# Eight-row loads for the first batch of a fused attention and GLU kernel, with squares moved to ScalarE and output weights loaded later

## The chip, the cores and the metric

The kernel runs on one core of one Trainium2 chip. The metric is the device time of one execution in microseconds (us), lower is better. Quoted times are medians of several runs. A traced run gives the profile and its own time; the profile's span, from the first to the last instruction, is some 2 us shorter than that time.

## The reference

Four batches of q, k and v, each 6016 rows by 256 columns in fp32. Per batch a channel attention of 256 by 256, then a gated feed-forward over all 24064 rows:

```python
qn = q / (np.linalg.norm(q, axis=1, keepdims=True) + 1e-06)     # norm over the 6016 rows
kn = k / (np.linalg.norm(k, axis=1, keepdims=True) + 1e-06)
s = kn.transpose(0, 2, 1) @ qn / tau                             # (B, 256, 256)
a = softmax(s)                                                   # written out in the original
x = (v @ a).reshape(B * N, C)
gate = 1.0 / (1.0 + np.exp(-(x @ w_gate)))                       # w_gate, w_val: 256 x 1536
return (gate * (x @ w_val)) @ w_out                              # w_out: 1536 x 256
```

## The kernel before

The rows of a batch are laid on 128 partitions, 47 rows each, and worked in groups of four rows ("four-row group": 128 partitions x 4 rows x 256, 512 KB of fp32 in HBM, cast to 256 KB of bf16 on the way). For the first batch nothing can overlap: all of q and k must land before its softmax is known. Then `a @ w_gate` and `a @ w_val` are formed (`gh`), and the feed-forward reads v directly. While batch b runs through the feed-forward, q and k of batch b+1 are loaded and their scores and squares are squeezed in as side work.

```python
TPC = 4                                      # rows of a group
NCH = (NT + TPC - 1) // TPC                  # 12 groups, NT = 47
groups0 = groups[: head // TPC] + [...]      # first batch: 11 groups of four, then rows 44-45, then row 46
qkpool = pool("qkpool", NCH)                 # slots for q and for k, four rows each
...
def load_qk(b, t0, nt):
    tiles = []
    for name, src in (("q", q), ("k", k)):
        tl = qkpool.tile([P, TPC, C], BF16, tag=name, name=name + "_sb")
        nc.gpsimd.dma_start(out=tl[:, :nt, :], in_=rows(src, b)[:, t0 : t0 + nt, :])
        tiles.append(tl)
    qk[b, t0] = tiles
...                                          # first group: two fp32 loads on other queues, cast on chip
for t0, nt in groups0[2:]:
    load_qk(0, t0, nt)
load_v(0, 0)
for fg in range(NFG):                        # gate and value weights, three pieces each, alternating
    for w, src in enumerate((moe_w_gate, moe_w_val)):
        nc.gpsimd.dma_start(out=w_sb[w][fg], in_=...)
load_v(0, 1)
nc.gpsimd.dma_start(out=w_out_sb, in_=moe_w_out.rearrange("(t p) c -> p t c", p=P))
...
for g, (t0, nt) in enumerate(groups0):       # first batch: squares, sums, scores
    engines = (nc.vector, nc.scalar) if g < last0 else (nc.scalar, nc.vector)
    sq = [squares(0, t0, nt, w, engines[w], ...) for w in range(2)]
    ...                                      # VectorE adds the squares up
    for u in range(nt):
        score(0, t0, u)
    if n_acc - 4 <= g < n_acc:
        busy(1)                              # a filler product on TensorE
...                                          # norms, softmax, busy(3), busy(1), first products gh(0, 0..4)
```

From there on a loop over chunks of v calls, at fixed places, the side work: `load_v` two chunks ahead, `transpose_v` (a DMA transpose of the next chunk from the SyncE queue, `vT<-v_sb`) one chunk ahead, and `load_qk` for the next batch about 20 of the loop's steps before use. A load waits on GpSimd until its slot is free (in the changed kernel GpSimd stood 5.26 us before the load at 74.63 us).

Of the kernel before, what the change touches and what calls it, by code (L numbers as in the profile page):

```python
# [10 lines left out]
BF16 = mybir.dt.bfloat16  # L11
# [6 lines left out]
def kernel(  # L18
# [20 lines left out]
    nc = tc.nc  # L39
    P = nc.NUM_PARTITIONS  # L40
# [4 lines left out]
    B, N, C = q.shape  # L45
# [7 lines left out]
    TPC = 4  # L53
    CH = TPC * P
    NCH = (NT + TPC - 1) // TPC
    groups = [(t, min(TPC, NT - t)) for t in range(0, NT, TPC)]

    head = NT - NT % TPC
    groups0 = groups[: head // TPC] + [(t, n) for t, n in ((head, NT % TPC - 1), (NT - 1, 1)) if n > 0]

    def rows(x, b):
        return x[b].rearrange("(p t) c -> p t c", p=P)
# [3 lines left out]
    def pool(name, bufs, **kw):  # L66
        return ctx.enter_context(tc.tile_pool(name=name, bufs=bufs, **kw))

    consts = pool("consts", 1)
    qkpool = pool("qkpool", NCH)  # L70
    sqpool = pool("sqpool", 3)
    attp = pool("attp", 1)
    ghpool = pool("ghpool", 2)
# [17 lines left out]
    qk = {}  # L91

    def load_qk(b, t0, nt):
        tiles = []
        for name, src in (("q", q), ("k", k)):
            tl = qkpool.tile([P, TPC, C], BF16, tag=name, name=name + "_sb")
            nc.gpsimd.dma_start(out=tl[:, :nt, :], in_=rows(src, b)[:, t0 : t0 + nt, :])  # L97
            tiles.append(tl)
        qk[b, t0] = tiles

    vs = {}

    def load_v(b, ci):
        t0, nt = groups[ci]
        v_sb = vpool.tile([P, TPC, C], BF16, tag="v", name="v_sb")
        nc.gpsimd.dma_start(out=v_sb[:, :nt, :], in_=rows(v, b)[:, t0 : t0 + nt, :])  # L106
        vs[b, ci] = v_sb


    t0, nt = groups0[0]  # L110
    qk[0, 0] = [qkpool.tile([P, TPC, C], BF16, tag=n, name=n + "_sb") for n in ("q", "k")]
    first_f32 = [consts.tile([P, nt, C], FP32, name=f"first{w}") for w in range(2)]
    for eng, tl, src in zip((nc.sync, nc.scalar), first_f32, (q, k)):
        eng.dma_start(out=tl, in_=rows(src, 0)[:, t0 : t0 + nt, :])
    nc.scalar.preload_act_table(ACT.Sqrt)
    load_qk(0, *groups0[1])

    ident_bf = consts.tile([P, P], BF16)
    make_identity(nc, ident_bf)
# [8 lines left out]

    nc.vector.tensor_copy(out=qk[0, 0][0], in_=first_f32[0])
    nc.scalar.copy(qk[0, 0][1], first_f32[1])  # L130
    for t0, nt in groups0[2:]:
        load_qk(0, t0, nt)
    load_v(0, 0)

# [1 line left out]
    w_out_sb = consts.tile([P, FC, C], BF16)  # L136
    for fg in range(NFG):
        for w, src in enumerate((moe_w_gate, moe_w_val)):
            nc.gpsimd.dma_start(
                out=w_sb[w][fg],  # L140
                in_=src.rearrange("(t p) f -> p t f", p=P)[:, :, ds(fg * FG, FG)],
            )
    load_v(0, 1)
    nc.gpsimd.dma_start(out=w_out_sb, in_=moe_w_out.rearrange("(t p) c -> p t c", p=P))


    st = {}
# [5 lines left out]
    def score(b, t0, u):  # L153
        q_sb, k_sb = qk[b, t0]
        if t0 == 0 and u == 0:
            st.setdefault(b, {})["s"] = pss.tile([P, CB, C], FP32, tag="s", name="ps_s")
        ps_s = st[b]["s"]
        t = t0 + u
        for j in range(CB):
            mm(  # L160
                ps_s[:, j, :],
                q_sb[:, u, ds(j * P, P)],
                k_sb[:, u, :],
                start=(t == 0 and j == 0),
                stop=(t == NT - 1),
                skip_group_check=True,
            )

    def squares(b, t0, nt, which, engine, sq=None):
        src = qk[b, t0][which]  # L170
        if sq is None:
            sq = sqpool.tile([P, TPC, C], BF16, tag=f"sq{which}", name=f"sq{which}")
        if engine is nc.scalar:
            nc.scalar.activation(out=sq[:, :nt, :], in_=src[:, :nt, :], func=ACT.Square)  # L174
        else:
            engine.tensor_tensor(  # L176
                out=sq[:, :nt, :], in0=src[:, :nt, :], in1=src[:, :nt, :], op=ALU.mult
            )
        return sq

    def norm_mms(ps, sqs, nt, first, last, order=(0, 1)):

        for w in order:
            sq = sqs[w]
            for u in range(nt):
                for j in range(CB):
                    mm(
                        ps[:, w * CB + j : w * CB + j + 1],
                        sq[:, u, ds(j * P, P)],
                        ones_bf[:, 0:1],  # L190
                        start=(first and w == order[0] and u == 0 and j == 0),
                        stop=(last and u == nt - 1),
                        skip_group_check=True,
                    )
# [276 lines left out]
    def busy(n):  # L471

        ps = psg.tile([P, CH], FP32, tag="g", name="ps_busy")
        for _ in range(n):
            mm(ps, ones_bf, ones_wide, True, True)
# [3 lines left out]
    n_acc = NT // TPC  # L479
    acc_start(0)  # L480
    acc = st[0]["acc"]
    last0 = len(groups0) - 1
    adds, ends = [], []
    for g, (t0, nt) in enumerate(groups0):
        engines = (nc.vector, nc.scalar) if g < last0 else (nc.scalar, nc.vector)
        sq = [squares(0, t0, nt, w, engines[w], acc[w] if g == 0 else None) for w in range(2)]
        while adds:
            w, last_sq = adds.pop()
            nc.vector.tensor_tensor(out=acc[w], in0=acc[w], in1=last_sq, op=ALU.add)
        if 0 < g < n_acc:  # L490
            nc.vector.tensor_tensor(out=acc[0], in0=acc[0], in1=sq[0], op=ALU.add)
            if g < n_acc - 1:
                nc.vector.tensor_tensor(out=acc[1], in0=acc[1], in1=sq[1], op=ALU.add)
            else:
                adds.append((1, sq[1]))
        elif g:
            ends.append((sq, nt))
        if g == last0:
            norm_mms(ps_n0, acc, TPC, True, False)
            for n, (end, rows_n) in enumerate(ends):  # L500
                norm_mms(ps_n0, end, rows_n, False, n == len(ends) - 1, (1, 0) if n else (0, 1))
# [3 lines that stand above are left out]
            busy(1)  # L505
# [28 lines left out]
    def side_work(b):  # L534


        side = {}

        def at(slot, fn, *a):
            side.setdefault(divmod(slot, FC), []).append((fn, a))  # L540

        for ci in range(NCH):
            nb, nci = (b, ci + 1) if ci + 1 < NCH else (b + 1, 0)
            lb, lci = (b, ci + 2) if ci + 2 < NCH else (b + 1, ci + 2 - NCH)
            if (nb, nci) == (0, 1):
                at(8, lambda: transpose_v(0, 1, psm.tile([P, TPC * CB, P], BF16, tag="m", name="ps_tp")))
            elif nb < B:
                at(ci * FC + 2, transpose_v, nb, nci)
            if lb < B:
                at(ci * FC + 0, load_v, lb, lci)  # L550
        n = b + 1
        if n == B:
            return side
        first, last = (14 if b == 0 else 0), 8 * FC
        for g, (t0, nt) in enumerate(groups):
            s0 = first + g * (last - first) // NCH
            at(max(0, s0 - 20), load_qk, n, t0, nt)
            for u in range(nt):
                at(first + (t0 + u) * (last - first) // NT, score, n, t0, u)
            if g == 0:  # L560
                at(s0, acc_start, n)
            for i, (fn, w) in enumerate(((acc_square, 0), (acc_add, 0), (acc_square, 1), (acc_add, 1))):
                at(s0 + 1 + 2 * i, fn, n, g, w)
        for i in range(6):
            at(8 * FC + 2 + i, acc_fold, n, *divmod(i, 3))
        at(9 * FC + 9, norms_mm, n)
        for ci, s, *call in (
            (9, 0, wide_sqrt, n),
            (9, 2, wide_inv, n, 0),
            (9, 3, wide_inv, n, 1),  # L570
            (10, 0, wide_scale, n),
            (10, 0, exps, n, 0),
            (10, 0, exps, n, 1),
        ):
            side.setdefault((ci, FC + s), []).append((call[0], call[1:]))
        at(11 * FC + 0, sums_both, n)
        at(11 * FC + 0, gh_tiles, n)
        for i in range(len(gh_order)):
            at(11 * FC + min(i + 1, FC - 1), gh, n, i, *((pss, "s"), (psm, "m"))[i % 2])
        return side  # L580
# [62 lines left out]
```

## Time and profile before

| | before |
|---|---|
| time, first three runs | 829.55 us (829.47 to 829.68) |
| time, all six runs beside the changed kernel | 829.62 us (829.47 to 829.97) |
| span of the traced run (829.76 us) | 827.7 us |
| TensorE busy | 806.9 us, 97% of the span |
| first gate product starts | 36.55 us |
| first output product starts | 53.94 us |

The page's first part (engine, busy time, share, instructions), a row of its second (40 slices of the span, the DMA engines' busy share in tenths) and one of its third (DMA queues: packets, MB, share of 16 engines):

```profile
PE 806.9 (97%) x5122; PEld 498.5 (60%) x5134; DVE 591.5 (71%) x1027; ACT 390.8 (47%) x642; POOL 83.1 (10%) x159
DMA  9999623226746443223876452223322323322211
...
q0 software_dynamic: 23920, 38.81, 28.1%
```

TensorE is nearly the whole span. The DMA row is full only in its first four slices, 83 us: up to about 48 us that is the first batch's q and k and the weights, and then mostly the second batch's q and k. q0 is GpSimd's queue of loads; the transposes and the stores go by another.

### The profile page before, as it was taken

The page shows a single profiled execution, that of the slowest core. Times are in us where ns is not written, and L with a number is a line of the kernel's source. Part 1 is how long each engine was busy: PE and PEld are TensorE (multiplying, and loading weights), DVE is VectorE, ACT ScalarE, POOL GpSimd, SP SyncE. Part 2 cuts the span into 40 slices and gives each one's busy share as a digit, 9 for nine tenths or more (in the row PEclk, how much of TensorE's full clock was granted, in tenths as well). Part 3 has the DMA queues.
Part 4 walks back from the last instruction along what each step waited for, and adds up shares of the span by engine and source line. Part 5 has one row for each costly group of instructions (what it writes and reads, how often), then busy time and mean ns, then how long its engine had stood idle before and what let it go on. Part 6 is the DMA issues. An engine that isn't in the chain of part 4 may idle for free.

```text
span 827.7 us, 13626 instructions
## 1 busy us (share of the span) xinstructions
PE 806.9 (97%) x5122; PEld 498.5 (60%) x5134; DVE 591.5 (71%) x1027; ACT 390.8 (47%) x642; POOL 83.1 (10%) x159
## 2 busy tenths in 40 slices
PE   4799999999999999999999999999999999999998
PEld 2456666665665666665575666666566566666666
DVE  6777877787667777778767777777766666666665
ACT  4554444446644444445654444444655444444442
POOL 5532100002210100000311010000000000000000
PEclk9899999999999999999999999999999999999999
DMA  9999623226746443223876452223322323322211
GB/s 210 206 201 216 110 52 90 60 53 136 158 88 119 96 89 61 54 52 85 158 138 124 80 107 60 51 63 75 64 61 63 73 52 85 60 58 69 47 36 71
DMA packets 79026, 77.17 MB, mean 93 GB/s; under 512 B 50800, under 2 KB 55920, under 8 KB 78960
## 3 DMA queue, kind: packets, MB, share of 16 engines
q0 software_dynamic: 23920, 38.81, 28.1%
q1 hardware_dynamic: 54752, 36.91, 17.4%
q8 instruction: 40, 0.66, 0.3%
q10 hardware_dynamic: 288, 0.59, 0.2%
q14 instruction: 26, 0.21, 0.1%
HBM read 78.64 MB, written 24.64 MB: 125 GB/s over the span
## 4 chain that ended last, share of the span: by engine, by line
PE 94%; DMA 4%; DVE 1%; issue 0%; ACT 0%; POOL 0%; POOLq 0%
PE ps_o L88 30%; PE ps_gate L88 29%; PE ps_val L88 29%; PE ps_s L88 4%; DMA k_sb<-in_k_dram 3%; PE ps_gh L88 2%; DMA w_gate<-in_moe_w_gate_dram 1%; DVE hT L426 0%; ACT g_sb L425 0%; PE ps_end L88 0%; DVE sq L176 0%; PE ps_n L88 0%; POOL q_sb L97 0%; PE ps_tp L396 0%; DVE end L467 0%
## 5 line engine op out<-in xcount | busy, mean ns | idle before, releaser
L426 DVE TENSOR_TENSOR hT<-ps_val,g_sb 128x512 bf16<-128x512 f32 (+1 forms) x576 | 390.8, 679 | 205.6 <-ACT g_sb L425 201.0
L425 ACT ACTIVATE g_sb<-ps_gate 128x512 bf16<-128x512 f32 (+1 forms) x576 | 338.2, 588 | 386.2 <-PE ps_gate L88 380.2
L88 PE MATMUL ps_val<-vT,gh_H 128*128 128x512 bf16 (+1 forms) x1152 | 337.6, 375 | 0.3
L88 PE MATMUL ps_gate<-vT,gh_G 128*128 128x512 bf16 (+1 forms) x1152 | 337.5, 375 | 0.2
L88 PE MATMUL ps_o<-w_out_sb,hT 128*128 128x256 bf16 x2244 | 324.9, 273 | 0.0
L88 PEld LDWEIGHTS <-hT 128*128 128x128 bf16 x2268 | 221.0, 98 | 124.6
L88 PEld LDWEIGHTS <-gh_H 128*128 128x128 bf16 x1152 | 112.7, 98 | 132.1 <-issue 1.4
L88 PEld LDWEIGHTS <-gh_G 128*128 128x128 bf16 x1152 | 112.4, 98 | 37.6 <-ACT gh_G L379 0.2
L106 POOL DMA_DIRECT2D v_sb<-in_v_dram x48 | 25.5, 531 | 620.2 <-DMA vT<-v_sb 480.4
L452 DVE COPY out_sb<-ps_o 128x256 f32<-128x256 f32 x187 | 77.2, 413 | 12.6 <-PE ps_o L88 12.6
L88 PE MATMUL ps_s<-k_sb,q_sb 128*128 128x256 bf16 x376 | 70.5, 289 | 15.8 <-DMA k_sb<-in_k_dram 8.8
L88 PEld LDWEIGHTS <-q_sb 128*128 128x128 bf16 x376 | 38.6, 103 | 24.6 <-issue 9.6
L215 DVE TENSOR_TENSOR acc<-acc,sq 128x1024 bf16<-128x1024 bf16 (+1 forms) x66 | 44.1, 669 | 0.0
L176 DVE TENSOR_TENSOR sq<-q_sb 128x1024 bf16<-128x1024 bf16 (+2 forms) x44 | 29.3, 667 | 0.0
L97 POOL DMA_DIRECT2D q_sb<-in_q_dram x48 | 26.5, 552 | 15.2 <-DMA q_sb<-in_q_dram 7.3
L97 POOL DMA_DIRECT2D k_sb<-in_k_dram x48 | 26.2, 545 | 16.1 <-DMA k_sb<-in_k_dram 6.6
L176 DVE TENSOR_TENSOR sq<-k_sb 128x1024 bf16<-128x1024 bf16 (+2 forms) x34 | 22.4, 658 | 0.2 <-DMA k_sb<-in_k_dram 0.2
L174 ACT ACTIVATE sq<-k_sb 128x1024 bf16<-128x1024 bf16 (+1 forms) x11 | 11.2, 1019 | 13.6 <-DMA k_sb<-in_k_dram 13.6
L88 PE MATMUL ps_gh<-w_val,e_sb 128*128 128x512 bf16 x45 | 13.5, 379 | 0.2
L88 PEld LDWEIGHTS <-e_sb 128*128 128x128 bf16 x112 | 10.2, 98 | 5.3 <-DMA w_gate<-in_moe_w_gate_dram 0.6
L88 PE MATMUL ps_gh<-w_gate,e_sb 128*128 128x512 bf16 x41 | 12.7, 379 | 0.7 <-DMA w_gate<-in_moe_w_gate_dram 0.5
L425 ACT ACT_TABLE_LOAD x6 | 7.7, 1283 | 9.0 <-PE ps_gate L88 9.0
(69 smaller groups left out, 121.1 us busy)
## 6 DMA issues: line engine op xcount, KB each, us to landing
out_dram<-out_sb SPq DMA_DIRECT2D x44, 512.0 KB, 2.9
v_sb<-in_v_dram POOLq DMA_DIRECT2D x44, 256.0 KB, 3.8
q_sb<-in_q_dram POOLq DMA_DIRECT2D x43, 256.0 KB, 7.4
k_sb<-in_k_dram POOLq DMA_DIRECT2D x43, 256.0 KB, 8.1
out_dram<-out_sb SPq DMA_DIRECT2D x3, 384.0 KB, 3.1
w_gate<-in_moe_w_gate_dram POOLq DMA_DIRECT2D x3, 256.0 KB, 8.0
w_val<-in_moe_w_val_dram POOLq DMA_DIRECT2D x3, 256.0 KB, 8.1
w_out_sb<-in_moe_w_out_dram POOLq DMA_DIRECT2D x1, 768.0 KB, 13.3
```

The lines of the kernel that those rows point to most:

```text
L88: nc.tensor.matmul(out, lhsT=lhsT, rhs=rhs, start=start, stop=stop, **kw)
L97: nc.gpsimd.dma_start(out=tl[:, :nt, :], in_=rows(src, b)[:, t0 : t0 + nt, :])
L106: nc.gpsimd.dma_start(out=v_sb[:, :nt, :], in_=rows(v, b)[:, t0 : t0 + nt, :])
L174: nc.scalar.activation(out=sq[:, :nt, :], in_=src[:, :nt, :], func=ACT.Square)
L176: engine.tensor_tensor(out=sq[:, :nt, :], in0=src[:, :nt, :], in1=src[:, :nt, :], op=ALU.mult)
L215: nc.vector.tensor_tensor(out=acc[:, :nt, :], in0=acc[:, :nt, :], in1=st[b]["sq", w][:, :nt, :], op=ALU.add)
L425: nc.scalar.activation(out=g_sb[:, :n], in_=ps_gate[:, :n], func=ACT.Sigmoid)
L426: nc.vector.tensor_tensor(out=hts[b, ci][:, f, :n], in0=ps_val[:, :n], in1=g_sb[:, :n], op=ALU.mult)
L452: nc.vector.tensor_copy(out=out_sb[:, s, :], in_=ps)
```

## The change

The intent: fewer and larger loads where the DMA queue is the bound; ScalarE takes over two squares so that VectorE is not behind when eight rows land at once; the output weights move out of the way of what is needed sooner. The core of the diff:

```diff
-    qkpool = pool("qkpool", NCH)
+    qkpool = pool("qkpool", 8)
...
-            tl = qkpool.tile([P, TPC, C], BF16, tag=name, name=name + "_sb")
+            tl = qkpool.tile([P, 2 * TPC, C], BF16, tag=name, name=name + "_sb")
             nc.gpsimd.dma_start(out=tl[:, :nt, :], in_=rows(src, b)[:, t0 : t0 + nt, :])
             tiles.append(tl)
-        qk[b, t0] = tiles
+        for u in range(0, nt, TPC):
+            qk[b, t0 + u] = [tl[:, u : u + TPC, :] for tl in tiles]
...
+    pairs = [(t, 2 * TPC) for t in range(TPC, head - 3 * TPC, 2 * TPC)]     # rows 4 to 35
+    loads0 = pairs + [(t, n) for t, n in groups0 if t >= pairs[-1][0] + 2 * TPC]
-    load_qk(0, *groups0[1])
+    load_qk(0, *loads0[0])
...
-    for t0, nt in groups0[2:]:
+    for t0, nt in loads0[1:]:
         load_qk(0, t0, nt)
...
-    nc.gpsimd.dma_start(out=w_out_sb, in_=moe_w_out.rearrange("(t p) c -> p t c", p=P))
+    def load_w_out():
+        nc.gpsimd.dma_start(out=w_out_sb, in_=moe_w_out.rearrange("(t p) c -> p t c", p=P))
...
-        engines = (nc.vector, nc.scalar) if g < last0 else (nc.scalar, nc.vector)
+        engines = [nc.vector, nc.scalar]
+        if n_acc - 2 <= g < n_acc:
+            engines[0] = nc.scalar
+        elif g == last0:
+            engines.reverse()
...                                          # in the loop's side work:
+            if (b, ci) == (0, 0):
+                at(0, load_w_out)
```

The slots grow to eight rows for every batch, and their number falls from 12 to 8. The later batches still load four rows at a time, so each of their loads fills half a slot.

More of the change, by code (lines that the diff above doesn't have):

```diff
@@ L110 @@
     t0, nt = groups0[0]
-    qk[0, 0] = [qkpool.tile([P, TPC, C], BF16, tag=n, name=n + "_sb") for n in ("q", "k")]
+    qk[0, 0] = [
+        qkpool.tile([P, 2 * TPC, C], BF16, tag=n, name=n + "_sb")[:, :TPC, :] for n in ("q", "k")
+    ]
     first_f32 = [consts.tile([P, nt, C], FP32, name=f"first{w}") for w in range(2)]
```

## The prediction

The forecast's sum came to -0.38 us for eight larger loads and 0 for the rest, 829.2 us; the 0.38 is what "moves ahead by that" means. How GpSimd paces its loads is shown by the trace of before: eight went out by 6.39 us without a wait for a landing, and the ninth, at 7.20, waited for that of the first q load.

> **What bounds the kernel now.** I read the page first, then the chain of waits in the first 62 us, then the order of instructions there, and last the DMA queues in short windows. TensorE carries 94% of the chain that ended last, and after 36.5 us it has nothing left to give: the stretches show it busy for 25.80 of 26.00 us and for 50.00 of 50.00.
>
> ```profile
> PE 94%; DMA 4%; DVE 1%; issue 0%; ACT 0%; POOL 0%; POOLq 0%
> 36.50:62.50 26.00, 25.80 (x140) 13.16 (x142) 18.24 (x30) 15.91 (x27) 9.11 (x18) 1.00 1.20 202
> 50.00:100.00 50.00, 50.00 (x322) 31.07 (x321) 37.51 (x64) 22.37 (x38) 11.63 (x22) 1.00 1.02 182
> ```
>
> The columns of the last two are stretch, its length, then busy time of PE, PE's weight load, DVE, ACT, POOL, the granted clock, DMA share and GB/s. All that the change touches is the 4% called DMA: the first batch's q and k, and then the weights. Its chain, as start, length and what:
>
> ```profile
> 1.89 6.29 DMA k_sb<-in_k_dram
> 8.18 0.28 issue
> 8.46 9.74 DMA k_sb<-in_k_dram
> 18.20 0.28 issue
> 18.48 9.74 DMA k_sb<-in_k_dram
> 28.22 0.28 issue
> 28.51 8.00 DMA w_gate<-in_moe_w_gate_dram
> 36.51 0.05 issue
> 36.55 0.60 PE ps_gh L88 x2
> ```
>
> [...]the hop from 8.46 to 18.48 is eight loads. Then the first gate weights land at 36.51 and the first product with them starts at 36.55. From there to the end TensorE is full, so the time of this one landing is what sets the total. How tight it is against the softmax beside it:
>
> ```profile
> PE ps_gh L88 <- DMA w_gate<-in_moe_w_gate_dram: 0.5, 1, 0.5
> 32.65 0.40 ACT L174 ACTIVATE sq<-q_sb 128x256 bf16<-128x256 bf16 x1
> 32.73 0.29 DVE L176 TENSOR_TENSOR sq<-k_sb 128x256 bf16<-128x256 bf16 x1 [0.16 <-DMA k_sb<-in_k_dram]
> 35.85 0.20 PE L88 MATMUL ps_r<-ones_bf,e_sb 128*128 128x1 bf16 x2 [0.35 <-ACT e_sb L316]
> 36.55 0.60 PE L88 MATMUL ps_gh<-w_gate,e_sb 128*128 128x512 bf16 x2 [0.49 <-DMA w_gate<-in_moe_w_gate_dram]
> ```
>
> The last k row lands at about 32.7, call it L. The squares, norms, square root and exponentials are over at 36.05, and then TensorE waits 0.5 us for the gate weights. So the softmax has 0.5 us of slack, and the queue has none.
>
> [...]eight loads of 512 KB of fp32 in 10.02 us (18.48 less 8.46) is 1.2525 us each, 418.6 GB/s read. (The page's 210 GB/s counts the bf16 bytes written, half of it.) [...]the granted clock falls to 0.5 at about 18.2 us and is back at 25.0[...].
>
> **The change, part by part.**
>
> *Runs of eight rows.* Sixteen four-row loads (rows 4 to 36 of q and of k) become eight eight-row loads; three four-row groups (the first, rows 36 and 40) and the tail of two rows and one row stay. Bytes are the same. A four-row load has 128 runs of 4 KB, the new one 128 runs of 8 KB. [...]The weight loads have the same bytes in 256 runs of 2 KB; from the issues that wait for them (37.76 to 44.10, five landings, four of them weights and one v) one takes (6.34 - 1.2525) / 4 = 1.272 us. So eight more runs on each engine cost 0.020 us, 2.4 ns each. [...]Everything behind them in the queue, v and the gate weights included, moves ahead by that, as the queue is never empty: its software row is at 112% of its engines' time from 8 us on, and with eight loads in flight in place of the same eight at half the size it is fuller yet. GpSimd's 0.53 us for an issue is off the path.
>
> *Two rows of groups arriving at once.* The last eight-row pair of k lands at L - 6.9 (backwards at 1.25 us a four-row tile: k40 at L - 1.9, q40 L - 3.1, k36 L - 4.4, q36 L - 5.6). VectorE needs 3 x 0.69 us a group (q's square, two sums), and must wait for ScalarE's squares of k at 1.04 us each. Without help it would be behind for the tail; that is what the second part is for. With ScalarE taking q's squares for rows 36 and 40, I lay out the two engines. ScalarE: k28 ends at L - 5.8, k32 L - 4.75, q36 L - 3.7, k36 L - 2.7, q40 L - 1.6, k40 L - 0.6, k44 (0.63) at L, q46 (0.40) L + 0.42, against L + 0.36 before (32.65 + 0.40). VectorE: row 32's second sum L - 3.0, row 36's sums L - 2.3 and L - 1.6, row 40's first L - 0.9, q44's square (0.43) L - 0.5, row 40's second sum L + 0.2, k46's square (0.29) L + 0.5, against L + 0.33. So the softmax starts about 0.16 us later after L. That comes out of its 0.5 us of slack, and 0.34 is left: it costs nothing.
>
> *Output weights later.* They go from before to after the third v load in the same queue, behind all gate and value weights in both cases. Before, they were issued at 34.32 and landed 13.3 us later, at 47.6; now[...] about 48.5. The first product that reads them starts at 54.1. Hidden, with 5 us to spare. No gain at the first gate weights either, as they were ahead already.
>
> *Buffers.* Eight slots of eight rows in place of twelve of four for the three later batches. Load g is asked for 20 of the loop's steps before its use, with groups about 7 to 8 steps apart, so three or four groups are ahead; the slot was freed eight groups before. No wait.
>
> Sum: -0.38 for the queue, 0 for the rest: 829.55 - 0.38 = 829.2 us.[...]
>
> **Rivals.** (a) *TensorE cold at the tail.* Its scores now come in bursts 5 us apart, 16 products of 0.13 us warm. Before, with 1.03 us of work in 2.5 us (41%), it fell cold at 18.2; cold, 8 products take 1.86 us. Bursts leave idle stretches of 3 us, so it will probably be cold before the last pair at 25.5. There 16 cold products and two filler products take some 4.6 us unbroken[...] If it stays cold throughout the softmax, 831. I give these 15% together. (b) *The transfer rate does not move*[...]: 829.3 to 829.6.[...] (d) *The output weights collide*, being needed at 54.1: that takes a delay of over 5 us, and speaks against itself. (e) *Another engine's delay holds the gate weights.* They landed at 36.51, about 1.1 us later than v's cadence would put them (L + 1.25 for v + 1.25 = 35.2), and one instruction fetch ran on a DMA engine then:
>
> ```profile
> q8 instruction: 1, 0.02, 5.8%
> ```
>
> That is in the window 34 to 35 us, 5.8% of 16 us or 0.93 us on a single engine[...]; if it falls elsewhere, the landing moves by up to 1 us earlier, and then the softmax binds, at a gain of 0.38 + 0.34 at most: 828.8.
>
> **Range and chances.** Runs of before spread over 0.2 us. [...]the cold TensorE is the tail on the slow side. Range 828.6 to 829.9. 2% would be 16.6 us, and the whole stretch that the change touches is 36.5 us[...]; neither side can give 16 us. Faster 0.01, same 0.98, slower 0.01.
>
> **What the changed profile would show.** Right: eight-row loads of k land 5.01 less 0.1 us apart; the last k row near 32.3; first gate weights near 36.1 and still the thing that the first product with them waits for, by about 0.3 us; output weights landing near 48.5 with no wait for them; the stretch from there on as before. Wrong: the first product waiting for the exponentials instead (the tail of squares or a cold TensorE), the cadence unchanged at 1.25 us per four rows, or a wait on q, k or output weights after 50 us.

## The result, and the profile after

| | before | changed |
|---|---|---|
| median of six runs | 829.62 us (829.47 to 829.97) | 829.82 us (829.21 to 830.27) |
| ratio | | 1.0001, 95% interval 0.9988 to 1.0014: same |
| traced run, and its span | 829.76, 827.7 | 830.27, 828.2 |
| first gate product | 36.55 | 36.19 |
| third weight product (`w_gate`, second piece) | 38.51, no wait | 38.57, waits 0.26 |
| first output product | 53.94 | 53.78 |
| TensorE's waits for a transpose | none | one, 0.5 us (0.8 on the weight load) |

A ratio here and below is the mean time of one kernel's fast runs over that of the other's runs of the same rounds, so not quite the ratio of the medians quoted. The predicted 829.2 (828.6 to 829.9) holds the median, but the six runs spread over 1.06 us, five times what the runs of before had shown, and the traced one is the slowest of them.

The prologue first. Two lines of the timeline before, the third weight product and the first output product:

```profile
38.51 0.59 PE L88 MATMUL ps_gh<-w_gate,e_sb 128*128 128x512 bf16 x2
...
53.94 0.60 PE L88 MATMUL ps_o<-w_out_sb,hT 128*128 128x256 bf16 x4
```

The timeline of the changed kernel (start, length, engine, line, operation, count, and the idle time before it with what ended it), the scores of the first and the fourth eight-row pair, then the last k row's square, then the products with weights and the first output product:

```profile
10.64 3.57 PE L88 MATMUL ps_s<-k_sb,q_sb 128*128 128x256 bf16 x16 [1.95 <-DMA k_sb<-in_k_dram]
...
25.32 2.12 PE L88 MATMUL ps_s<-k_sb,q_sb 128*128 128x256 bf16 x16 [1.55 <-DMA k_sb<-in_k_dram]
...
32.32 0.29 DVE L184 TENSOR_TENSOR sq<-k_sb 128x256 bf16<-128x256 bf16 x1 [0.16 <-DMA k_sb<-in_k_dram]
...
36.19 0.60 PE L88 MATMUL ps_gh<-w_gate,e_sb 128*128 128x512 bf16 x2 [0.54 <-DMA w_gate<-in_moe_w_gate_dram]
...
38.57 0.59 PE L88 MATMUL ps_gh<-w_gate,e_sb 128*128 128x512 bf16 x2 [0.26 <-DMA w_gate<-in_moe_w_gate_dram]
...
53.78 0.60 PE L88 MATMUL ps_o<-w_out_sb,hT 128*128 128x256 bf16 x4
```

A pair of eight-row loads lands every (25.32 - 10.64) / 3 = 4.89 us, 2.45 us a load, against 2 x 1.2525 = 2.505 for two four-row loads in before. The last k row's square starts at 32.32 instead of 32.73, and the first gate product at 36.19 instead of 36.55. That is the predicted gain. But the second piece of `w_gate`, which before was there when TensorE came to it, is now waited for: of the 0.36 us nothing is left at 38.57 against 38.51, and 0.16 us at the first output product (53.78 against 53.94).

The chain that ended last in the changed kernel, from the page by shares of the span:

```profile
PE 92%; DMA 6%; DVE 1%; issue 0%; POOL 0%; ACT 0%; POOLq 0%
```

and piece by piece (start, length, what):

```profile
15.74 14.56 DMA k_sb<-in_k_dram
...
30.59 7.94 DMA w_gate<-in_moe_w_gate_dram
...
38.57 0.59 PE ps_gh L88 x2
...
72.62 14.98 DMA vT<-v_sb
```

It runs through the second piece of `w_gate` in place of the first. And a new link stands at 72.62: the DMA transpose of the fourth chunk of v, whose product is reached 15 us later. DMA's share of the chain is up from 4% to 6%. What waits for the transpose, from the timeline of the changed kernel:

```profile
87.64 0.60 PE L88 MATMUL ps_gate<-vT,gh_G 128*128 128x512 bf16 x2 [0.52 <-DMA vT<-v_sb]
```

The transpose was issued and landed 10.8 us later before, 15.0 after. Stretches of the two kernels (stretch, length, busy time of PE, PE's weight load, DVE, ACT, POOL, then granted clock, DMA share and GB/s), before:

```profile
78.00:82.00 4.00, 4.00 (x28) 2.63 (x27) 3.17 (x6) 1.57 (x3) 0.00 (x0) 1.00 1.17 209
...
86.00:90.00 4.00, 4.00 (x27) 2.51 (x26) 3.26 (x7) 1.79 (x3) 0.71 (x2) 1.00 1.06 196
```

and after:

```profile
78.00:82.00 4.00, 4.00 (x29) 2.52 (x27) 3.16 (x6) 1.46 (x4) 0.00 (x0) 1.00 1.38 95
...
86.00:90.00 4.00, 3.48 (x22) 1.88 (x20) 3.00 (x6) 1.39 (x3) 1.59 (x3) 1.00 0.26 28
```

TensorE loses 0.52 of 4 us at 86 to 90. From 78 to 82 the DMA engines are more occupied than before (1.38 against 1.17) but move 95 GB/s instead of 209: the packets themselves take longer. By the DMA view of that stretch a packet of the load queue took 329 ns on average instead of 151, and one of the queue of transposes and stores 80 instead of 32. What feeds them is seen on GpSimd, before:

```profile
71.42 0.53 POOL L97 DMA_DIRECT2D k_sb<-in_k_dram  x1 [0.72 <-ACT g_sb L425]
84.07 0.53 POOL L106 DMA_DIRECT2D v_sb<-in_v_dram  x1 [12.12 <-DMA vT<-v_sb]
```

and after:

```profile
68.84 0.53 POOL L98 DMA_DIRECT2D k_sb<-in_k_dram  x1 [0.68 <-DVE sq L184]
74.63 0.53 POOL L98 DMA_DIRECT2D q_sb<-in_q_dram  x1 [5.26 <-DVE hT L434]
75.15 0.54 POOL L98 DMA_DIRECT2D k_sb<-in_k_dram  x1
88.12 0.53 POOL L108 DMA_DIRECT2D v_sb<-in_v_dram  x1 [12.44 <-DVE hT L434]
```

Before, GpSimd issued the last of its loads at 71.42, ahead of the transpose. After, it stands 5.26 us, by the experiments below for want of a free slot, and issues a pair at 74.63 and 75.15, behind the transpose and into it. These two took 11.8 and 12.5 us to land.

### The profile page after: what moved, and what is told of

It is laid out like the page before. It is cut to its first block, busy times and chain, and to the rows that moved or that the text cites. A ratio compares the mean times of both kernels' runs of the same rounds, so it can differ in the third digit from the quotient of the medians.

```text
span 828.2 us, 13621 instructions
## 1 busy us (share of the span) xinstructions
PE 807.9 (98%) x5122; PEld 499.1 (60%) x5134; DVE 590.2 (71%) x1025; ACT 392.2 (47%) x644; POOL 78.9 (10%) x151
## 3 DMA queue, kind: packets, MB, share of 16 engines
q0 software_dynamic: 22768, 38.81, 28.5%
## 4 chain that ended last, share of the span: by engine, by line
PE 92%; DMA 6%; DVE 1%; issue 0%; POOL 0%; ACT 0%; POOLq 0%
PE ps_o L88 29%; PE ps_gate L88 29%; PE ps_val L88 29%; PE ps_s L88 4%; DMA k_sb<-in_k_dram 3%; PE ps_gh L88 2%; DMA vT<-v_sb 2%; DMA w_gate<-in_moe_w_gate_dram 1%; DVE hT L434 0%; DVE sq L184 0%; PE ps_end L88 0%; ACT g_sb L433 0%; POOL q_sb L98 0%; PE ps_n L88 0%; POOL k_sb L98 0%
## 5 line engine op out<-in xcount | busy, mean ns | idle before, releaser
L88 PE MATMUL ps_s<-k_sb,q_sb 128*128 128x256 bf16 x376 | 71.2, 293 | 14.6 <-DMA k_sb<-in_k_dram 7.6
L98 POOL DMA_DIRECT2D q_sb<-in_q_dram x44 | 24.2, 549 | 38.5 <-PE ps_s L88 12.4
L98 POOL DMA_DIRECT2D k_sb<-in_k_dram x44 | 24.0, 544 | 14.5 <-DMA k_sb<-in_k_dram 7.7
## 6 DMA issues: line engine op xcount, KB each, us to landing
k_sb<-in_k_dram POOLq DMA_DIRECT2D x4, 512.0 KB, 13.4
```

The lines of the kernel that those rows point to most:

```text
L88: nc.tensor.matmul(out, lhsT=lhsT, rhs=rhs, start=start, stop=stop, **kw)
```

## The experiments

Theory A: the eight slots hold GpSimd's loads back until they travel with the transpose, which then lands too late for TensorE; the prologue gains what was predicted. Rivals: the later output weights push the transpose (B); TensorE was cold at the tail, rival (a) of the prediction; the instruction fetch moved, rival (e); or the squares on ScalarE are what costs or gains. The experiments ran in three groups of four, each with the kernel before beside it (the record gives chip 0 for e1 to e8, chip 8 for e9 to e12, and no chip for the first six runs): 829.54 us (829.34 to 830.16) for e1 to e4, 829.57 (829.36 to 829.81) for e5 to e8, 829.57 (829.38 to 829.72) for e9 to e12. All results were correct.

### e1_after_again: the changed kernel, unaltered, once more

> The changed kernel unaltered, for more runs and a second trace. Its first six runs lay between 829.21 and 830.27 us. In the trace at hand the first gate product starts 0.36 us earlier than before (36.19 against 36.55 us) and then TensorE stands still once, before 87.6 us, for the transpose of the fourth v chunk, which took 15.0 us from issue to landing (10.8 before). Theory A (eight q and k slots: the loads of the second batch's later groups must wait for a slot and fall into that transpose) and rival B (the output weights' new place in the queue) both expect the same here: first gate product near 36.2, runs spread over 829.2 to 830.3, and in the traced run a wait on that transpose of 0 to 1.4 us that makes up the difference of its span from 827.1.

Measured: 829.06 us (829.02 to 829.08), ratio 0.9994 (0.998 to 1.0007). The transpose took 13.4 us and nobody waited for it. The first gate product started at 36.03, the second piece of `w_gate` was in use at 38.24, the first output product at 53.45, 0.49 us ahead of before. The spread and the wait that were expected did not come. So the same program has two outcomes, with and without the wait at 87 us, and without it the gain is in the total, though inside the noise of the ratio.

### e2_halves: sixteen groups ahead instead of eight

In the later batches two four-row groups share one eight-row slot.

```diff
+    whole = {}
     def load_qk(b, t0, nt):
+        second = b > 0 and t0 // TPC % 2 == 1
         for w, (name, src) in enumerate((("q", q), ("k", k))):
-            tl = qkpool.tile([P, 2 * TPC, C], BF16, tag=name, name=name + "_sb")
+            if second:
+                tl = whole[w][:, TPC:, :]
+            else:
+                tl = qkpool.tile([P, 2 * TPC, C], BF16, tag=name, name=name + "_sb")
+                whole[w] = tl
```

> The changed kernel, but in the later batches two four-row groups share one eight-row slot, so sixteen groups can be in flight in place of eight. Same memory. Theory A: the second batch's loads no longer wait for a slot, the transpose of the fourth v chunk lands in about 11 us as before, TensorE has no wait on it, and all runs lie at 829.2 (829.1 to 829.4), spread below 0.3. Rival B (order of the output weights): the wait stays, runs spread over 829.2 to 830.3 as for the changed kernel. Rival C (chance, unrelated to the slots): like B.

Measured: 829.14 us (829.11 to 829.40), ratio 0.9995 (0.9983 to 1.0008). GpSimd's loads ran as before the change, the last at 70.81 and the next at 83.70:

```profile
70.81 0.53 POOL L104 DMA_DIRECT2D k_sb<-in_k_dram  x1 [0.73 <-DMA k_sb<-in_k_dram]
83.70 0.53 POOL L114 DMA_DIRECT2D v_sb<-in_v_dram  x1 [12.36 <-DMA vT<-v_sb]
```

The transpose took 10.6 us. That is what A asks for. The traced run, the slowest of the five at 829.40, showed something else besides. Its stretches, in the columns given above:

```profile
28.00:30.00 2.00, 2.00 (x11) 1.19 (x10) 2.00 (x4) 2.00 (x3) 1.36 (x2) 0.50 1.11 202
30.00:32.00 2.00, 2.00 (x13) 1.46 (x12) 1.89 (x4) 1.56 (x3) 1.46 (x3) 0.69 1.30 200
```

The granted clock, third from the right, is 0.50 at 28 to 30 us where e1 has 1.00. TensorE worked through without a pause and was late with its norm products; the first gate product started at 36.38 with no wait for the weights, and the first output product at 53.76, 0.31 us behind e1. This is rival (a), at a cost of 0.3 us; the four other runs, at 829.11 to 829.18, were probably without it: their recorded mean clock is 0.996 to 1.000, that of the traced run 0.993.

### e3_wout_back: output weights at their old place

```diff
-    def load_w_out():
-        nc.gpsimd.dma_start(out=w_out_sb, in_=moe_w_out.rearrange("(t p) c -> p t c", p=P))
+    nc.gpsimd.dma_start(out=w_out_sb, in_=moe_w_out.rearrange("(t p) c -> p t c", p=P))
...
-            if (b, ci) == (0, 0):
-                at(0, load_w_out)
```

> The changed kernel with the output weights issued where they were before, ahead of the third v load. Theory A: no different from the changed kernel, a spread of 829.2 to 830.3 and q's loads still waiting for slots at about 74 us. Rival B: steady 829.2, no wait on the transpose of the fourth v chunk.

Measured: 829.32 us (829.1 to 830.37; the other four within 829.42), ratio 0.9999 (0.9986 to 1.0011). The transpose took 13.2 us, as in e1. So B falls: the order of the output weights doesn't lengthen the transpose, and the time is the same within the noise. The one run at 830.37 was not traced.

### e4_before_8slots: the kernel before with eight slots

```diff
-    qkpool = pool("qkpool", NCH)
+    qkpool = pool("qkpool", 8)
```

> The kernel before, with eight slots of four rows for q and k in place of twelve, nothing else. Theory A: the transfers of the first batch are as before (first gate product at 36.5), but the second batch's loads now wait for slots and the transpose of the fourth v chunk is late in some runs: 829.5 to 830.6, with a wider spread than before's 0.5. Rival B: like before, 829.5 to 829.9. If the first batch's own loads lose time to eight slots, the first gate product would start later than 36.6, which neither expects.

Measured: 829.43 us (829.38 to 829.66), ratio 0.9999 (0.9986 to 1.0012). The transpose took 13.7 us instead of 10.8, and GpSimd stood 5.08 us and then issued a pair at 74.70:

```profile
69.09 0.53 POOL L97 DMA_DIRECT2D k_sb<-in_k_dram  x1 [0.68 <-DVE sq L176]
74.70 0.53 POOL L97 DMA_DIRECT2D q_sb<-in_q_dram  x1 [5.08 <-DVE hT L426]
```

No product waited, and the late runs and the wider spread that A expected did not come. So it is the number of slots that lengthens the transpose, without any eight-row load; at 13.7 it is still in time. That the slots alone lead to a wait is not shown.

### e5_sq_back: q's squares of the last two groups back on VectorE

```diff
-        if n_acc - 2 <= g < n_acc:
-            engines[0] = nc.scalar
-        elif g == last0:
+        if g == last0:
             engines.reverse()
```

> The changed kernel with q's squares for rows 36 and 40 back on VectorE. By the layout in the prediction VectorE then has 2 x 0.69 us more to do after the last pair, so k46's square ends about 1.4 us later than now (33.9 in place of 32.6), the first gate product starts when the softmax is done and not when the weights land, at about 37.0 us in place of 36.15, and the time is 829.9 (829.6 to 830.3). If the prediction's claim that the squares are hidden is wrong and VectorE never was behind, nothing changes: 829.1.

Measured: 830.04 us (829.85 to 830.19), ratio 1.0006 (0.9994 to 1.0019). From the timeline:

```profile
33.20 0.35 PE L88 MATMUL ps_n<-ones_bf,acc 128*128 128x1 bf16 x8 [0.59 <-DVE acc L499]
...
36.48 0.59 PE L88 MATMUL ps_gh<-w_gate,e_sb 128*128 128x512 bf16 x2
```

The norm products wait for VectorE's sum, and the first gate product starts at 36.48 with its weights there. (37.0 was expected; the last k row's square came at 33.06 instead of 33.9.) The first output product starts at 53.87, 0.42 us behind e1. In this run the transpose took 14.9 us and TensorE's weight load waited 0.7 for it. So the ScalarE squares are needed: without them the softmax takes back the queue's gain. That the total met the expected 829.9 or so is in part luck, as it holds the wait for the transpose.

### e6_gate_later: one v load moved ahead of the weights

The second v load stands before the gate and value weights, so each of these lands one load later.

```diff
     load_v(0, 0)
+    load_v(0, 1)
...
-    load_v(0, 1)
```

> The changed kernel with the second v load moved from behind the gate and value weights to ahead of them: one four-row load (1.25 us) more in front of the weights, same bytes in all. If the landing of the weights sets the total, as the prediction has it, the first gate product starts 1.25 us later, at 37.4, and the time is 830.3 (830.1 to 830.5). If the softmax or TensorE's own work sets it, less than 0.7 us is lost: below 829.8.

Measured: 830.64 us (830.3 to 831.56), ratio 1.0018 (1.0004 to 1.0032). The timeline shows three waits on weights:

```profile
36.87 0.60 PE L88 MATMUL ps_gh<-w_gate,e_sb 128*128 128x512 bf16 x2 [1.08 <-DMA w_gate<-in_moe_w_gate_dram]
38.15 1.02 PE L88 MATMUL ps_gh<-w_val,e_sb 128*128 128x512 bf16 x4 [0.19 <-DMA w_val<-in_moe_w_val_dram]
39.47 0.59 PE L88 MATMUL ps_gh<-w_gate,e_sb 128*128 128x512 bf16 x2 [0.30 <-DMA w_gate<-in_moe_w_gate_dram]
```

The first gate product was expected at 37.4 and came at 36.87, 0.84 us behind e1 and not one load. But 39.47 against 38.24 in e1 is 1.23 us, one load, and the three runs at 830.30 to 830.64 are 1.24 to 1.58 us above e1's 829.06. So the landing of the weights sets the total, and the piece that decides is the third of them as much as the first. The two runs at 831.5 were not traced and stay unexplained.

### e7_slots7 and e11_slots7_again: seven slots

```diff
-    qkpool = pool("qkpool", 8)
+    qkpool = pool("qkpool", 7)
```

> The changed kernel with seven slots of eight rows in place of eight. Theory A (loads that must wait for a slot fall into the transpose of the fourth v chunk and draw it out: 10.6 to 10.8 us where they did not wait, in the kernel before and with halves, 13.2 to 15.0 in the four traces where they did): two loads more are held back, the transpose takes 14 us or longer, and TensorE waits on it in most runs, 829.3 to 831. Rival (the length of that transpose is chance, or comes from the runs of eight rows themselves): 13 to 15 us again and 829.1 without a wait in most runs.

> Seven slots again, beside the changed kernel on the same chip. With seven the transpose of the fourth v chunk took 5.9 us, not 14 or more as theory A said: the load that waits for a slot came at 74.1 us, but the queue ahead had run dry by then and the transpose went through first. If that is how it works: 829.0, no run above 829.4. If the 5.9 was luck: runs up to 830.3, as with eight.

Measured: 829.06 us (828.93 to 829.33), ratio 0.9995 (0.9983 to 1.0008), and 829.05 us (828.83 to 829.45), ratio 0.9994 (0.9981 to 1.0008). The transpose took 5.9 us both times. So the dose in theory A, fewer slots and a longer transpose, fell, and so did its rival of 13 to 15 us again. GpSimd in the first of the two:

```profile
65.82 0.53 POOL L108 DMA_DIRECT2D v_sb<-in_v_dram  x1 [0.28 <-DMA v_sb<-in_v_dram]
74.12 0.53 POOL L98 DMA_DIRECT2D q_sb<-in_q_dram  x1 [7.77 <-DVE hT L434]
```

With one slot fewer it stops a pair of loads earlier, at 65.82, and fewer loads travel beside the transpose: from 74 to 76 us the load queue's packets took 24% of the engines' time, in the changed kernel 101%. Seven slots have the transpose done 8 us before its use. By this reading eight is the number at which GpSimd's backlog and the next pair both meet it; that is argued from these traces, and no other number was run.

### e8_halves_warm: e2 with eight filler products more before the tail

```diff
-        if n_acc - 4 <= g < n_acc:
-            busy(1)
+        if n_acc - 6 <= g < n_acc:
+            busy(4 if g < n_acc - 4 else 1)
```

> Two groups to a slot as in the second experiment, and four filler products after each of the fifth and sixth groups, so that TensorE is kept from falling to half clock before the tail. In the trace of the second experiment it was cold from 24 to 31 us, the first gate product started at 36.51 for it, and that run took 829.40 where the four others took 829.11 to 829.18. If the cold tail is what cost that run, here the granted clock is 1.00 from 28 us on, the first gate product starts at 36.1 to 36.2, and all five runs lie within 829.0 to 829.2. If the fillers delay the scores instead: the first gate product later than 36.3 and 829.3 or more.

Measured: 829.86 us (829.11 to 830.92), ratio 1.0006 (0.9994 to 1.0019). The traced run, 830.79, shows where it went:

```profile
33.63 0.29 DVE L190 TENSOR_TENSOR sq<-k_sb 128x256 bf16<-128x256 bf16 x1 [1.44 <-DMA k_sb<-in_k_dram]
```

The last k row came 1.3 us later than in the changed kernel (32.32). An instruction fetch (queue q8, one packet, 5.6% of the 16 engine-us of the stretch 31 to 32 us, which is 0.9 us on one DMA engine) ran there; in before and in the changed kernel a fetch of that size started at 34.4 and 34.0. The load before that row landed as in the changed kernel (32.0). TensorE then idled, its clock fell to a mean of 0.62 at 34 to 37 us, and the first gate product started at 37.41. So in this run the fetch of rival (e) came ahead of the last row.

### e9_early_fillers: the same number of fillers at the very start, where TensorE is idle

```diff
+    busy(8)
     ps_n0 = psm.tile([P, 2 * CB], FP32, tag="m", name="ps_n")
```

> The changed kernel with eight filler products at the very start, where TensorE stands idle until 6.8 us: sixteen TensorE instructions (eight products with their weight loads) more ahead of the tail, as in the eighth experiment, but no work near it. There the one instruction fetch of the first 37 us came at 31.5 us in place of 33.9, ahead of the last k row, which landed at 33.6 in place of 32.3. If it is the count of instructions that moves the fetch, and the fetch that delays the row: the fetch comes before 32.5 us again, k46's square starts at 33 or later, and the time is 829.4 to 830.9. If the eighth experiment's fillers cost by their own work near the tail: fetch at 33.9, k46's square at 32.3, 829.1 (or up to 830.3 if the transpose of the fourth v chunk is waited for).

Measured: 830.51 us (829.9 to 830.92), ratio 1.001 (0.9998 to 1.0023). One line of its DMA queues in the stretch 31 to 31.5 us (queue, packets, MB, share of 16 engines), and from its timeline the last k row:

```profile
q8 instruction: 1, 0.02, 12.2%
```

```profile
33.39 0.29 DVE L184 TENSOR_TENSOR sq<-k_sb 128x256 bf16<-128x256 bf16 x1 [1.37 <-DMA k_sb<-in_k_dram]
```

12.2% of 16 x 0.5 us is 0.98 us on one engine. The fetch is at 31 to 31.5 us and the row 1.07 us late, now with fillers that run when TensorE has nothing else. In e8 and e9 alike, sixteen TensorE instructions more came with an earlier fetch and a late row, wherever the fillers stood, and the loads before that row were on time. That the fetch delays it fits both runs. What places the fetch is not shown: the trace has some 264 TensorE instructions started before it in the changed kernel, 202 in e8, 184 here and 252 in e10, so it is no fixed count of started ones. (The clock was also at 0.50 from 24 to 30 us in this run, but the row's wait is for its DMA.) The first gate product starts at 36.53, without a wait for the weights. The transpose took 14.6 us here and TensorE's weight load waited 0.5 for it.

### e10_no_fillers: without the sixteen filler instructions

```diff
-        if n_acc - 4 <= g < n_acc:
-            busy(1)
...
-    busy(3)
...
-    busy(1)
```

> The changed kernel without its eight filler products in the tail: sixteen instructions fewer. If the count moves the fetch, it comes later than 34.5 us, the first gate weights land before it, and the first gate product starts at 35.6 or as soon as the softmax is done. Against that, TensorE has less to do after 25 us and may be at half clock in the tail, which costs up to 0.5 us as in the second experiment. 828.8 if the clock stays up, 829.5 if not.

Measured: 830.23 us (828.97 to 830.35), ratio 1.0003 (0.9991 to 1.0016), in two clusters: 828.97 and 829.30, and 830.23, 830.25, 830.35. The traced run is of the second. The fetch stayed at 33.5 to 34 us: fewer instructions did not move it by as much as half a microsecond, against what was expected if their count placed it. Its stretches:

```profile
36.00:38.00 2.00, 1.95 (x7) 0.80 (x8) 0.98 (x3) 0.55 (x2) 1.57 (x2) 0.62 1.24 206
38.00:40.00 2.00, 2.00 (x6) 0.73 (x5) 0.75 (x1) 1.17 (x3) 0.62 (x2) 0.53 1.24 204
```

TensorE started its first gate product at 35.99 but at half clock, and reached the first output product at 54.65, 1.20 us behind e1. So without the fillers the clock falls just where the path begins to be TensorE's. The two fast runs were not traced, so whether their clock stayed up is not shown. The recorded mean clock doesn't settle it: 1.000 for 828.97, but 0.996 for 829.30, as for two of the three slow ones.

### e12_after_third: the changed kernel a third time

> The changed kernel unaltered, for its spread on one more chip: 829.05 (the second time) to 830.3 (the first). In the traces with eight slots the transpose of the fourth v chunk took 13.2 to 15.0 us and TensorE waits for it from about 14.3 on. If the trace shows under 14 us, all runs should be 829.0 to 829.3; if over 14.3, a wait on it and 829.5 to 830.3.

Measured: 829.25 us (829.14 to 829.43), ratio 0.9997 (0.9984 to 1.0009). The transpose took 13.4 us, with no wait; first gate product 36.00, first output product 53.39. It agrees with e1, not with the first six runs.

### All traces in one table

If the argument is right, a run's span is the start of the first output product, plus one constant for the rest, plus what TensorE waited for the transpose. The remainder is the span less that start. (The span is taken because the time is 1.87 to 2.12 us longer than it, which would blur the sum.)

| traced run | time | span | first output product | remainder | transpose, us | weight load waits for it |
|---|---|---|---|---|---|---|
| before | 829.76 | 827.7 | 53.94 | 773.76 | 10.8 |  |
| changed | 830.27 | 828.2 | 53.78 | 774.42 | 15.0 | 0.8 |
| e1 changed again | 829.07 | 827.2 | 53.45 | 773.75 | 13.4 |  |
| e2 halves | 829.40 | 827.5 | 53.76 | 773.74 | 10.6 |  |
| e3 output weights back | 829.12 | 827.1 | 53.40 | 773.70 | 13.2 |  |
| e4 before, 8 slots | 829.66 | 827.6 | 53.86 | 773.74 | 13.7 |  |
| e5 squares back | 830.12 | 828.2 | 53.87 | 774.33 | 14.9 | 0.7 |
| e6 weights later | 830.36 | 828.4 | 54.68 | 773.72 | 9.9 |  |
| e7 seven slots | 829.06 | 827.0 | 53.28 | 773.72 | 5.9 |  |
| e8 halves, warm | 830.79 | 828.9 | 55.13 | 773.77 | 9.2 |  |
| e9 early fillers | 830.08 | 828.0 | 53.91 | 774.09 | 14.6 | 0.5 |
| e10 no fillers | 830.25 | 828.4 | 54.65 | 773.75 | 10.1 |  |
| e11 seven slots | 829.16 | 827.1 | 53.41 | 773.69 | 5.9 |  |
| e12 changed, third | 829.22 | 827.1 | 53.39 | 773.71 | 13.4 |  |

Eleven runs without the wait have remainders of 773.69 to 773.77. The three with it have 774.09, 774.33 and 774.42, in the order of their waits, and these are the three whose transpose took over 14 us. So the prologue and this one wait account for every traced span to about 0.1 us.

## Why the prediction was right or wrong, point by point

**Bound by the landing of the first gate weights.** Right in direction, too narrow. e6 delays all weights by one load and the traced run grows by one load. But the step "the time of this one landing is what sets the total" named only the first of six pieces. In the changed kernel the second piece of `w_gate` is waited for as well (0.26 us at 38.57), and this landing decides. In e1 and e12 it came at 38.24 and 38.17 and the gain stayed; in the first traced run at 38.57 and most of it was gone. What moved it by 0.3 us between runs of one program is open. It isn't the larger loads that bring this second wait: e4, with loads of four rows, waits 0.26 us for the same piece at 38.64.

**Runs of eight rows, -0.38 us.** Right: an eight-row load took 2.45 us against 2.505 for two four-row loads, and 0.36 to 0.55 us at the first gate product (36.19, 36.03, 36.00 against 36.55). The rate is the firm part: eight loads save 8 x (2.505 - 2.45) = 0.44 us, and e4, with four-row loads, started its first gate product at 36.34, so some 0.2 us of the start is scatter. Rival (b), no change of rate, is out by the same number. A load's packets did not grow in number with its rows: sixteen four-row loads were 2304 packets before (8.18 to 28.22 us), 144 each, and the load queue has 23920 - 22768 = 1152 fewer after, 144 for each of the eight loads saved. The 2.4 ns a run that the prediction took from the times of issues is less sure: the landings of four weight pieces (37.19 to 42.32 in before) give some 3.7. What part of the 0.055 us a load saved is for runs and what for the load itself was not shown.

**The squares.** Right that they cost nothing and are needed: 0.54 us of slack after, where 0.34 was expected; without them (e5) the first output product comes 0.42 us later than in e1.

**Output weights later.** Right: issued at 36.4 and landed 12.4 us on, at 48.8 (48.5 predicted), unused until 53.8. e3 shows the order makes no difference.

**"Buffers. [...] No wait."** This is the step that failed. I counted slots by the program's steps, 20 ahead of use, and found three or four groups in flight. GpSimd runs far ahead of those steps, held by free slots (the 5.26 us below) and by earlier landings (in before the ninth load, at 7.20 us, waited for that of the first): when before issued its last load at 71.42, ten groups of the second batch were issued and TensorE was at the scores of the second. With eight in place of twelve it stopped after nine (68.84), stood 5.26 us, then issued a pair into the transpose, which grew from 10.8 to 15.0 us in the traced run and cost a 0.5 us stop of TensorE, 0.7 us in the remainder (774.42 against 773.75 and 773.71 in e1 and e12). e4 and e2 show from both sides that the slots lengthen the transpose (13.7 with eight in the kernel before, 10.6 with sixteen groups in the changed one); the stop itself came in three of the traces with eight slots and not in six others. I had listed "a wait on q, k or output weights after 50 us" as a sign of being wrong; the wait came on v, one queue further.

**Rivals.** (a), a cold TensorE, came in e2 (0.3 us) and in a run without fillers (1.2 us), and the clock was down for a while in e8 (0.62 on average at 34 to 37 us) and e9 (0.50 at 24 to 30 us) too; the traced runs of the changed kernel were warm by the tail (1.00 at 30 to 34 us). (e), the fetch, stayed where it was in the changed kernel. In e8 and e9, where it came earlier, the first output product was 0.5 us or more later (55.13 and 53.91 against 53.45 and 53.39; in e8 half clock had a part in it). But (e) had a point: in both the first gate product no longer waited for its weights (0.54 us in the changed kernel), and in e9 TensorE's last wait before it was 0.36 us for the exponentials, so the softmax bound there, as (e) said. (Its "about 1.1 us later" is a slip: 36.51 less 35.2 is 1.3.) (d) did not occur.

**The total.** 829.82 us lies in the range, but by two things against each other: in two later sets of runs, without the wait in their traces, the same kernel ran 829.06 and 829.25, -0.48 and -0.32 us against before, about the predicted gain; of the first six most gave it back. So that the median lies in the range is in part luck. That the untraced runs of the first six, of which two were at 829.2, fall into the same two groups is likely by the table but not shown; their recorded mean clock doesn't part them (1.000 for 830.27 and for 829.21). Whether the chip makes the difference is open as well. Runs of the changed kernel at a first output product of 53.4 us had the transpose at 13.4, and those delayed to 53.8 or 53.9 (changed, e5, e9) at 14.6 to 15.0; delayed further, to 54.65 (e10), it was 10.1. So the timing of the prologue seems to decide how badly loads and transpose collide; that is read off these traces and not tested, and e4 (53.86, but 13.7) doesn't fit it. The rule behind that, and why packets take longer in the collision, stay open.

The best version was seven slots: 829.05 and 829.06 us, some 0.5 us below before, with 8 us of room for the transpose. It is inside the noise of the ratio, and nothing to claim but the robustness. Twelve slots of eight rows were not run; e2 stands in for them.

## What to carry to other kernels

When a pool's number of slots changes, ask what paces the queue that fills it: here GpSimd, which issues the loads, ran ahead until it lacked a slot (the last load before its long stand went out at 71.42 us with twelve slots, 68.84 with eight, 65.82 with seven), so the slot count decided when the loads started and which other transfer they met. Where a landing sets the total, look at the next landings behind it too: here 0.36 us gained at the first gate product became 0.16 us at the first output product, with a wait of 0.26 us for the third weight product in between. And to explain tenths of a microsecond, split each traced run at a point where the bound changes; here one start time, a constant and one wait accounted for all fourteen spans.

## What else the traces show

- The 46 DMA transposes of before landed 3.7 us after their issue in the median (3.3 to 16.0); that of the fourth chunk landed after 5.9 us with seven slots, and after 9.2 to 15.0 us among q and k loads in the other traces. In the changed kernel the engines were then, from 78 to 82 us, 138% occupied by the profile and moved 95 GB/s, against 209 in the same stretch before.
- One instruction fetch (0.02 MB in the profile) was 0.9 to 1.0 us on a DMA engine. In e8 and e9, where it came some 2.5 us earlier, the last k row landed 1.1 to 1.3 us late.
- GpSimd's loads ran far ahead of their use: in the changed kernel nine groups of the second batch were issued by 68.84 us, with the second in use. In that trace, with eight slots in place of twelve, GpSimd then stood 5.26 us and TensorE 0.5 us.
